# A fourth pair of token blocks takes the seven-product form in the first MLP

## The chip, the core and the metric

The kernel runs on one core of a Trainium2 chip. The metric is device time in microseconds, start to end of one execution, lower is better. A core has TensorE (PE in the profile, its weight loads are PEld), VectorE (DVE), ScalarE (ACT), GpSimd (POOL) and SyncE (SP, whose queue issues nearly all DMAs here), each with an instruction stream of its own that runs in order; streams wait for each other on semaphores.

## What is computed

Three stages on 6016 tokens of 256 channels, float32 throughout:

```python
qn = q / (norm(q, axis=tokens) + 1e-6); kn = k / (norm(k, axis=tokens) + 1e-6)
a  = softmax(kn.T @ qn / tau)              # 256 x 256
x  = v @ a                                 # attention
h  = maximum(x @ w_in, 0)                  # 256 -> 2048
x  = (h * h) @ w_out                       # first MLP, 2048 -> 256
xn = x / sqrt(mean(x * x) + 1e-6) * rms_g
out = (silu(xn @ w_gate) * (xn @ w_val)) @ w2   # second MLP, d_ff 1536
```

## The kernel before

Float32 products are made of three matmuls on high and low halves (high x high, high x low, low x high; `mm3`, L109 to L112). So every operand has to be split: ACT rounds to the high half, DVE subtracts to get the low half. Weights are also converted from their raw bits in several small steps (class `Call`: POOL and ACT in `a`, three DVE operations in `b0`, `b1`, `b2`, then `h` on ACT and `l` on DVE).

The attention matrix is folded into the first weight: M = a @ w_in, 256 x 2048, in halves m_h and m_l. `emit_m(fc)` makes M in eight parts of 256 columns, beside the first blocks. The first MLP is then relu(v @ M) squared, times w_out.

Tokens lie in 12 blocks: ten of 512 and two of 448. Two forms of the first MLP exist:

- **Ordinary blocks** (`mlp1`, L863). A block has 16 units, one for each 128 columns of M. In a unit PE makes `up(f)`: 6 matmuls into one of four banks; ACT takes relu (L870), a square (L874) and a rounded copy (L875), DVE subtracts for the low half (L882); where `act_heavy` is false the square is DVE's (L877) and ACT writes the rounded square at once (L878). Three units later PE makes `down(f)`, 6 matmuls into the block's sums. Blocks 0 and 1 are interleaved (32 units, numbered x), since the weights arrive meanwhile; later blocks follow one by one.
- **Pairs** (`mlp1_pair`, L1357). Two blocks together form the product with M from seven block products in place of eight (Strassen's scheme in Winograd's form). A pair has 8 groups; a group is 7 products of 3 matmuls and 24 matmuls of down. It needs sums of M's quarters (`comb_steps`, L1178) and seven operands made from the pair's v (`v_steps`, L1238).

`FIRST = NP - 3` (L56) puts blocks 0 to 5 into the ordinary form and pairs 3, 4 and 5 (blocks 6 to 11) into the other. The second MLP has the pair form for all six pairs.

All work beside PE's is placed by hand into units and groups. Lists by unit: `hooks` run ahead of the unit's relu, `beside` behind its subtraction. In blocks 2 to 4 (`CONV`) one conversion step (`conv_steps`) and at listed units one step of M's sums (`COMB`) stand beside each unit. `norm_steps(b)` (s0 to s6) is the RMS norm of a finished block, `pair_steps(p)` makes and stores the seven operands of the second MLP for a pair, `prep(b)` transposes and splits the next block's v. `third` (beside block 5) rounds the last of M's sums. In a pair, `aside()` runs after three of the products in each group: it takes one step from the list `side` (norms, `pair_steps`) and one from `tokens` (the next pair's `v_steps`); in the pair numbered FIRST a staged token step is held back where the side step just run was staged too (`staged` in `aside`).

`v_steps` has two forms. Pair FIRST + 1 goes through tiles vraw and vt. Later pairs are `wide`: their v is loaded (`load_v`, L465) at the end of the pair two before them into place p0 and the tile gv1, is worked on in gv1, and each operand goes through DRAM (v_dram). `fetch_v` brings an operand back: for a wide pair the first three into gv1, else into p6, vt and vraw; the other four into raw and dg.

Of the second MLP's gate and value weights a chunk (256 columns, seven operands) is 1.75 MB. Before, chunk 0 is converted in the blocks beside `CONV` and kept in gv0; chunk 1 (`STREAMED`) is converted beside the last pair (`last_chunk`), stored to DRAM and loaded into gv1 behind it.

Of the kernel before, what the change touches and what calls it, by code (L numbers as in the profile page):

```python
# [20 lines left out]
P = 128  # L21
NB = 512
# [6 lines left out]
def attn_moe_kernel(ctx: ExitStack, tc, q, k, v, tau, w_in, w_out, w_gate, w_val, w2, rms_g, out):  # L29
# [25 lines left out]
    NP = NBLK // 2  # L55
    FIRST = NP - 3  # L56

# [129 lines left out]
    NGV = F2 // W2  # L187
    HELD = 1
    EARLY = 1
# [6 lines left out]
    def gv_pool(i):  # L196
        return [(wp, "gv0"), (wp, "gv1"), (mp, "m_h"), (mp, "m_l"), (wp, "wo_h"), (wp, "wo_l")][i]

# [6 lines left out]
    class Pieces(Call):  # L205
# [5 lines left out]
        def direct(self):  # L211
            return self.i < HELD or self.i > STREAMED

# [77 lines left out]
    class Value(Pieces):  # L291
# [17 lines left out]
        def b2(self):  # L309
            super().b2()  # L310
            a2 = self.g.rearrange("p (k w) -> p k w", k=KC)
            s = self.raw.bitcast(F32).rearrange("p (c w) -> p c w", w=W2)
            self.pieces = [(a2[:, 1:], 2, 1), (s[:, :2], 3, 2), (s[:, 2:], 5, 2)]
            if self.i < STREAMED:
                for part in range(2):
                    self.sums(nc.gpsimd.tensor_tensor, part)
# [99 lines left out]

    gv_calls = [c for i in range(STREAMED) for c in chunk_calls(i)]
    w2_calls = [Rows2(rows2(w2, i), i) for i in range(EARLY)]
# [761 lines left out]
    def comb_steps():  # L1180
# [11 lines left out]
        def tt(o, a, b, op):  # L1192
            def f():
                if not comb:
                    tile3()
                x, y = (comb["t"][:, i] if isinstance(i, int) else m(*i) for i in (a, b))
                nc.vector.tensor_tensor(out=comb["t"][:, o], in0=x, in1=y, op=op)

            return f

        def hi(k, o):
            return lambda: nc.scalar.copy(out=comb["h"][:, k], in_=comb["t"][:, o])

        def lo(k, o):
            return lambda: nc.vector.tensor_tensor(
                out=comb["l"][:, k], in0=comb["t"][:, o], in1=f32(comb["h"])[:, k], op=ALU.subtract
            )
# [14 lines left out]
        ]  # L1222
        return steps, third

# [12 lines left out]
    def v_steps(p, into):  # L1237
# [7 lines left out]
        def loads(t):  # L1245
            def f():
                home = None
                if wide:
                    if t == 0:
                        x = wp.tile([P, NC7, NB], F32, tag="gv1", name="vx")  # L1250
                        st["raw"] = x[:, 5:]
                        st["x"] = {i: x[:, k, :n] for k, i in enumerate((0, 4, 2, 6, 3, 1, 5))}
                    home = (place(0, F32), st["raw"])[t]
                raw[t] = load_v(b + t, home)

            return f
# [90 lines left out]
    def fetch_v(p, i, ops):  # L1347

        n = blocks[2 * p][1]
        k = ORDER.index(i)  # L1350
        if k < 3 and p > FIRST + 1:
            if k == 0:
# [422 lines left out]
    ys = {b: parts[b][2] for b in (0, 1)}  # L1775
    n0, n1 = norm_steps(0, ys[0])
    for x, (b, f) in enumerate(order):
        up, down, _ = parts[b]
        beside = conv_steps(1) if x >= at0[NT] else ()
        unit(lambda: up(f), lambda down=down, f=f: down(f), 2 if x < 10 else 3, hooks.get(x, ()), late.get(x, ()), (), beside)  # L1780

    UNITS = 16
    CONV = range(2, 2 * FIRST - 1)

    cstep, third = comb_steps()
    SKIP = {2: (4, 10), 3: (4, 6, 9, 12), 4: (1, 5, 9, 11, 13)}
    COMB = {2: (2, 4, 6, 10, 14), 3: (0, 2, 12, 13, 14), 4: (2, 8, 9, 10, 11, 12)}


    ops1 = {}  # L1790
    spill = {}
    for b in range(2, 2 * FIRST):
        hooks, beside = spill, {}
        spill = {}

        if b == 2:
            hooks = merge({1: n0, 2: n1[:1], 3: n1[1:2], 4: n1[2:3]}, {6: n1[3:4], 7: n1[4:5], 8: n1[5:6], 9: n1[6:]})
            n0, n1 = norm_steps(1, ys[1])
            hooks = merge(hooks, {10: n0, 11: n1[:1], 12: n1[1:2], 13: n1[2:3]})
            spill = {0: n1[3:4], 1: n1[4:5], 2: n1[5:6], 3: n1[6:]}  # L1800
        else:
            n0, n1 = norm_steps(b - 1, ys[b - 1])
            if b == 2 * FIRST - 1:
                hooks = merge(hooks, *({u: [f]} for u, f in zip((8, 9, 10, 11, 13, 14, 15, 15), n0 + n1)))
            elif b % 2:
                hooks = merge(hooks, {13: n0, 14: n1[:1], 15: n1[1:2]})
                spill = {0: n1[2:3], 3: n1[3:4], 4: n1[4:5], 5: n1[5:6], 6: n1[6:]}
            else:
                hooks = merge(hooks, {7: n0, 8: n1[:1], 9: n1[1:2], 10: n1[2:3], 13: n1[3:4], 14: n1[4:5], 15: n1[5:]})
        if b > 2 and b % 2:  # L1810
            x = pair_steps(b // 2 - 1, staged("ys", "p0", "ys", "p1"))
            beside = merge(beside, at_steps(x, {3: 4, 2 * FIRST - 1: 0}.get(b, 1)))
        if b < 2 * FIRST - 1:
            x = prep(b + 1)
            hooks = merge(hooks, {0: [load(b + 1)]} if b > 2 else {})
            at = (8, 9, 12, 13) if b == 3 else (8, 9, 10, 11) if b % 2 else (3, 4, 8, 9)
            beside = merge(beside, {u: [f] for u, f in zip(at, x)})
        else:
            beside.setdefault(0, []).append(third)
            x = v_steps(FIRST, first_place(ops1))  # L1820
            for u in (0, 1, 3, 5, 6, 7, 8, 9, 10, 11, 11, 12, 13, 14, 15):
                beside.setdefault(u, []).append(x.pop(0))
        for u in range(UNITS):
            if b in CONV:
                if u not in SKIP.get(b, ()):
                    beside.setdefault(u, []).extend(conv_steps(1))
                if u in COMB.get(b, ()):
                    beside.setdefault(u, []).append(cstep.pop(0))
            beside.setdefault(u, []).append(lambda: None)
        up, down, ys[b] = mlp1(b, vts[b], (lambda f: f % 4 > 0) if b in CONV else (lambda f: f % 2 == 1))  # L1830
        run(up, down, NF1, 3, hooks, {}, beside)
        if b == CONV[-1]:
            left = [len(list(x)) for x in (conv, cstep)]
            assert left == [0, 0] and state["b"] == len(calls) == state["l"], left
# [65 lines left out]
    def last_homes():  # L1900
        halves = place(1, F32)
        last_chunk.update(
            chunk_steps(
                STREAMED,
                (
                    lambda: (as_raw(place(0, F32)), halves[:, 1]),
                    lambda: (as_raw(place(6, F32)), halves[:, 0]),
                ),
                None,
                lambda t=staged("p0", "vt"): t().rearrange("p a (c w) -> p a c w", w=W2),  # L1910
            )
        )
# [31 lines left out]
    side, tokens = [], []  # L1944
    drained.append(lambda: side.extend(n0 + n1 + pair_steps(FIRST - 1, first_stage)))
    first_stage = staged(*["ys", "p6", "ys"] * 4, "ys", "ys")
    for p in range(FIRST, NP):
# [9 lines left out]
        elif first:  # L1957
            tokens += v_steps(p + 1, through_dram(p + 1, stage))
            wide_steps = v_steps(p + 2, through_dram(p + 2, staged("p1", "p0")))
        else:  # L1960
            tokens += wide_steps

        def after_product(g, i):
            if g == NF1 // 2 - 1:
                if not last and i in ORDER[3:]:
                    fetch_v(p + 1, i, nxt)
                if last and i == 0:
                    fetch(0, 4, ops0, False)
                if p == FIRST and i == ORDER[-1]:
                    wide_steps.pop(0)()  # L1970
                    wide_steps.pop(0)()
                if p == NP - 2 and i == 0:
                    last_chunk["vload"]()

        def after_group(g):
# [4 lines left out]
            if not last and g == NF1 // 2 - 2:  # L1980
# [3 lines left out]
                if p == NP - 2:  # L1984
                    last_homes()
                    last_chunk["gload"]()
                    tokens.extend([bridge.a, bridge.b, None])
            if last:
                if g == NF1 // 2 - 3:
                    rows[f"{STREAMED + 1}gload"]()  # L1990
                if g == NF1 // 2 - 2:
# [52 lines left out]
    for i in range(STREAMED + 1, NGV):  # L2044
# [7 lines left out]

        if not early:
            add(f"{x}gload", (f"{j - 1}c", 0))
        add(f"{x}ga", (f"{x}gload", LAND), (f"{y}ve", 0), (f"{y}gl0", 0))
# [6 lines left out]
        for b, a, lag in (("b", "a", 2), ("c", "b", 1), ("h", "c", 2), ("l", "h", 1)):  # L2062
            add(f"{j}{b}", (f"{j}{a}", lag))
        if not early:
            add(f"{x}vload", (f"{y}vl2", 0))
        add(f"{x}va", (f"{x}vload", LAND), (f"{y}vl0", 0))
        for b, a, lag in (
# [3 lines left out]
            add(f"{x}{b}", (f"{x}{a}", lag), *([(f"{x}gc", 0)] if b == "vd" else [(f"{x}vl1", 0)] if b == "vl2" else []))  # L2071
    flow.at.update({f"{STREAMED + 1}gload": 0, f"{STREAMED + 1}vload": 0})
    side = []
# [10 lines left out]
    for x, (p, span) in enumerate(visits):  # L2084
# [7 lines left out]
        def after_group(f):  # L2092
            if x == 0:
                if f == 0:
                    load_w2(ROWS, 2)
                    rows[f"{STREAMED + 1}vload"]()
                if f == 1:
# [75 lines left out]
```

## Time and profile before

| | us |
|---|---|
| median of 3 executions | 1110.95 (1110.93 to 1111.2) |
| the profiled execution | 1110.91 |
| its span, first to last instruction | 1109.0 |
| PE busy | 1099.5 |
| DVE busy | 808.0 |
| ACT busy | 787.0 |

The profile shows one execution; times within it are counted from its first instruction. The busy time of PE counts the pipelined run of each matmul, so it says only that PE always has a matmul under way; how closely they follow each other is read from their starts.

### The profile page before, as it was taken

How to read it: one execution, taken by the hardware profiler on the slowest of the kernel's cores; microseconds unless marked ns; L12 is line 12 of the kernel's file. 1: busy time of each engine (PE TensorE's matmuls, PEld its weight loads, DVE VectorE, ACT ScalarE, POOL GpSimd, SP SyncE). 2: the span in 40 equal slices, each digit the busy share in tenths (PEclk: the TensorE clock that was granted, in tenths of full speed). 3: DMA queues.
4: the chain of work that ended last, by engine and by line, in shares of the span. 5: the costliest groups of instructions: out<-in, count | busy, mean ns of one | idle time of the engine just before them, and what ended most of it. 6: DMA issues, size and time to landing. Idle time of an engine off the chain costs nothing.

```text
span 1109.0 us, 14698 instructions
## 1 busy us (share of the span) xinstructions
PE 1099.5 (99%) x5148; PEld 928.0 (84%) x5148; DVE 808.0 (73%) x1266; ACT 787.0 (71%) x1430; POOL 39.1 (4%) x74
## 2 busy tenths in 40 slices
PE   9999999999999999999999999999999999999997
PEld 8978888888888888889988888888888888888996
DVE  7988768667777868979858888677556666565655
ACT  7888788787777778778777777676656555555554
POOL 2021101000000000000000000000000000000000
PEclk9999999999999999999999999999999999999999
DMA  9643210130411362461385656204323232404001
GB/s 346 214 114 96 87 47 20 48 105 1 135 56 58 143 219 50 152 253 39 129 325 226 226 197 220 72 9 169 133 73 133 77 133 54 149 21 122 20 20 33
DMA packets 113177, 130.98 MB, mean 118 GB/s; under 512 B 51664, under 2 KB 73168, under 8 KB 112976
## 3 DMA queue, kind: packets, MB, share of 16 engines
q1 hardware_dynamic: 110832, 129.20, 34.7%
q10 hardware_dynamic: 2272, 0.85, 0.3%
q8 instruction: 40, 0.66, 0.2%
q14 instruction: 33, 0.27, 0.1%
HBM read 87.43 MB, written 42.60 MB: 117 GB/s over the span
## 4 chain that ended last, share of the span: by engine, by line
PE 96%; DMA 2%; DVE 1%; SPq 1%; ACT 0%; issue 0%; DVEq 0%; ACTq 0%
PE mm L1548 30%; PE acc L111 13%; PE acc L110 13%; PE acc L112 13%; PE mm L1416 9%; PE mm L112 4%; PE mm L111 4%; PE mm L110 4%; PE mm L663 1%; PE acc L671 1%; PE acc L672 1%; PE acc L673 1%; PE mm L796 1%; DMA vr<-vd 1%; DMA qraw<-in_k_dram 0%; SPq L1163 0%
## 5 line engine op out<-in xcount | busy, mean ns | idle before, releaser
L1548 PE MATMUL mm<-p,gv 128*128 128x512 f32 (+1 forms) x1188 | 302.0, 387 | 0.0
L1548 PEld LDWEIGHTS mm<-p,gv 128*128 128x128 f32 x1188 | 222.0, 188 | 44.8 <-DVE hp L1628 1.0
L1653 DVE TENSOR_TENSOR sh<-hp,sh 128x512 fp32r<-128x512 f32 (+1 forms) x144 | 98.8, 686 | 111.8 <-ACT sh L1649 110.8
L1603 ACT COPY mm<-mm 128x512 f32<-128x512 f32 (+1 forms) x72 | 40.4, 562 | 159.7 <-PE mm L1548 154.9
L110 PE MATMUL acc<-sh,wo_h 128*128 128x512 f32 (+1 forms) x384 | 148.6, 387 | 0.0
L111 PE MATMUL acc<-sh,wo_h 128*128 128x512 f32 (+1 forms) x384 | 148.3, 386 | 0.1
L112 PE MATMUL acc<-sh,wo_l 128*128 128x512 f32 (+1 forms) x384 | 148.0, 385 | 0.0
L882 DVE TENSOR_TENSOR sh<-p,sh 128x512 fp32r<-128x512 f32 x96 | 67.1, 698 | 58.7 <-ACT sh L875 55.0
L110 PE MATMUL acc<-sh,w_h 128*128 128x512 f32 (+1 forms) x284 | 109.5, 385 | 0.0
L111 PE MATMUL acc<-sh,w_h 128*128 128x512 f32 (+1 forms) x284 | 109.5, 385 | 0.0
L112 PE MATMUL acc<-sh,w_l 128*128 128x512 f32 (+1 forms) x284 | 109.5, 385 | 0.0
L1649 ACT CAST sh<-hp 128x512 fp32r<-128x512 f32 (+1 forms) x144 | 89.0, 618 | 2.8 <-DVE hp L1637 1.9
L870 ACT ACTIVATE p<-mm 128x512 f32<-128x512 f32 x96 | 57.2, 596 | 41.7 <-PE mm L112 41.4
L111 PEld LDWEIGHTS acc<-sh,wo_h 128*128 128x128 f32 x384 | 72.1, 188 | 13.9 <-DVE sh L1406 0.7
L112 PEld LDWEIGHTS acc<-sh,wo_l 128*128 128x128 f32 x384 | 72.1, 188 | 13.6
L110 PEld LDWEIGHTS acc<-sh,wo_h 128*128 128x128 f32 x384 | 72.1, 188 | 13.3
L1548 PE MATMUL mm<-xs,gv 128*128 128x512 f32 (+1 forms) x324 | 82.6, 381 | 0.0
L1637 DVE TENSOR_TENSOR hp<-mm,sg 128x512 f32<-128x512 f32 (+1 forms) x72 | 48.8, 678 | 34.1 <-PE mm L1548 33.5
L1406 DVE TENSOR_TENSOR sh<-p,sh 128x512 fp32r<-128x512 f32 (+1 forms) x95 | 63.5, 668 | 13.7 <-ACT p L1401 5.5
L1548 PEld LDWEIGHTS mm<-xs,gv 128*128 128x128 f32 x324 | 60.8, 188 | 10.2
L1628 DVE TENSOR_TENSOR hp<-mm,pu 128x512 f32<-128x512 f32 (+1 forms) x72 | 48.9, 680 | 27.6 <-ACT pu L1627 27.5
L1397 ACT ACTIVATE sh<-p 128x512 fp32r<-128x512 f32 (+1 forms) x95 | 58.4, 615 | 9.3 <-DVE p L1466 7.3
(285 smaller groups left out, 2182.9 us busy)
## 6 DMA issues: line engine op xcount, KB each, us to landing
p<-xd SPq DMA_DIRECT2D x102, 256.0 KB, 4.6
xd<-xp SPq DMA_DIRECT2D x48, 256.0 KB, 2.2
xs<-xd SPq DMA_DIRECT2D x12, 512.0 KB, 5.8
xd<-p SPq DMA_DIRECT2D x22, 256.0 KB, 2.2
out_dram<-ot SPq DMA_DIRECT2D x40, 128.0 KB, 2.3
qraw<-in_q_dram SPq DMA_DIRECT2D x13, 384.0 KB, 7.1
qraw<-in_k_dram SPq DMA_DIRECT2D x13, 384.0 KB, 7.6
raw<-in_moe_w_out_dram SPq DMA_DIRECT2D x9, 512.0 KB, 3.5
```

Of the source, the lines that this page charges most:

```text
L110: nc.tensor.matmul(o, wh, xh, start=start, stop=False)
L111: nc.tensor.matmul(o, wh, xl, start=False, stop=False)
L112: nc.tensor.matmul(o, wl, xh, start=False, stop=stop)
L870: nc.scalar.activation(out=r, in_=o, func=AF.Relu)
L882: nc.vector.tensor_tensor(out=sl, in0=s, in1=f32(sh), op=ALU.subtract)
L1397: nc.scalar.activation(out=st["h"], in_=r, func=AF.Square)
L1406: nc.vector.tensor_tensor(out=st["l"], in0=q, in1=f32(st["h"]), op=ALU.subtract)
L1416: nc.tensor.matmul(bank, m_part(a, w, g), x, start=start and j == 0, stop=j == 2, skip_group_check=not start)
L1548: nc.tensor.matmul(bank, c[:, hl, a, fs], x, start=start and j == 0, stop=j == 2, skip_group_check=not start)
L1628: add(out=h22, in0=bh, in1=w, op=ALU.add)
L1649: nc.scalar.copy(out=parts[t][0], in_=x)
L1653: dve(out=pl, in0=x, in1=f32(ph), op=ALU.subtract)
```

## The change

FIRST becomes NP - 4: blocks 0 to 3 are ordinary, pairs 2 to 5 have the seven products. What stood beside blocks 2 to 5 has to go elsewhere:

- The sixteen steps of M's sums are split in halves of 512 columns (32 steps, `gs`). The first fourteen stand beside units x = 18 to 31 of blocks 0 and 1, the other eighteen beside block 2. All sixteen conversion steps are done by the end of block 2.
- Block 2 takes the norm of block 0 and three parts of four of block 1's; block 3 takes the rest of it, `pair_steps(0)` (through two staging tiles, `kept(2)`, in place of four), the beginning of block 2's norm, and pair 2's `v_steps`. The rest of block 2's norm (`kept_steps`) goes to the side list of pair 2.
- Pairs 4 and 5 are wide now; pair 4 has gv1 and pair 5 has gv0. So gv0 can't hold a chunk over the first MLP: chunk 1 is the one that is converted beside the blocks and goes through DRAM, into gv0 behind the last pair, and chunk 0 is converted beside the last pair, straight into gv1.
- Chunk 2's loads, which used vt and vraw (now operands of pair 5), move to the beginning of the second MLP.

```diff
-    FIRST = NP - 3
+    FIRST = NP - 4
...
-        return [(wp, "gv0"), (wp, "gv1"), (mp, "m_h"), (mp, "m_l"), (wp, "wo_h"), (wp, "wo_l")][i]
+        return [(wp, "gv1"), (wp, "gv0"), (mp, "m_h"), (mp, "m_l"), (wp, "wo_h"), (wp, "wo_l")][i]
...
-            return self.i < HELD or self.i > STREAMED
+            return self.i != STREAMED
...
-    gv_calls = [c for i in range(STREAMED) for c in chunk_calls(i)]
+    gv_calls = list(chunk_calls(STREAMED))
...
-            def f():
+            def f(gs):
                 if not comb:
                     tile3()
-                x, y = (comb["t"][:, i] if isinstance(i, int) else m(*i) for i in (a, b))
-                nc.vector.tensor_tensor(out=comb["t"][:, o], in0=x, in1=y, op=op)
+                x, y = (comb["t"][:, i, gs] if isinstance(i, int) else m(*i)[:, gs] for i in (a, b))
+                nc.vector.tensor_tensor(out=comb["t"][:, o, gs], in0=x, in1=y, op=op)
...
-        return steps, third
+        return [lambda f=f, gs=gs: f(gs) for gs in (slice(0, G // 2), slice(G // 2, G)) for f in steps], third
...
-                        x = wp.tile([P, NC7, NB], F32, tag="gv1", name="vx")
+                        x = wp.tile([P, NC7, NB], F32, tag=f"gv{(p - FIRST + 1) % 2}", name="vx")
...
-        if k < 3 and p > FIRST + 1:
+        if k < 3 and (p - FIRST) % 2 == 0:
...
+    cstep, third = comb_steps()
+    COMB0 = range(18, NU)
...
+        if x in COMB0:
+            beside = [*beside, cstep.pop(0)]
+            if x < at0[NT]:
+                beside.append(lambda: upto("h", state["b"]))
...
     for b in range(2, 2 * FIRST):
+        last = b == 2 * FIRST - 1
+        beside = {}
+        if not last:
+            n0, n1 = norm_steps(0, ys[0])
             hooks = merge({1: n0, 2: n1[:1], 3: n1[1:2], 4: n1[2:3]}, {6: n1[3:4], 7: n1[4:5], 8: n1[5:6], 9: n1[6:]})
             n0, n1 = norm_steps(1, ys[1])
             hooks = merge(hooks, {10: n0, 11: n1[:1], 12: n1[1:2], 13: n1[2:3]})
             spill = {0: n1[3:4], 1: n1[4:5], 2: n1[5:6], 3: n1[6:]}
+            beside = merge(beside, {u: [f] for u, f in zip((3, 4, 8, 9), prep(b + 1))})
+            for u in range(UNITS):
+                beside.setdefault(u, []).extend(conv_steps(1))
+                beside[u] += [cstep.pop(0) for _ in range(1 + (u in (5, 15)))]
         else:
...
+            n0, n1 = norm_steps(2, ys[2])
+            hooks = merge(spill, {13: n0, 14: n1[:1], 15: n1[1:2]})
+            kept_steps = n1[2:]
+            spill = {}
+            beside = merge(beside, at_steps(pair_steps(0, kept(2)), 4))
             beside.setdefault(0, []).append(third)
             x = v_steps(FIRST, first_place(ops1))
...
-        up, down, ys[b] = mlp1(b, vts[b], (lambda f: f % 4 > 0) if b in CONV else (lambda f: f % 2 == 1))
+        up, down, ys[b] = mlp1(b, vts[b], lambda f: f % 4 > 0)
...
-    drained.append(lambda: side.extend(n0 + n1 + pair_steps(FIRST - 1, first_stage)))
+    side.extend(kept_steps)
+    drained.append(lambda: (side.insert(0, n0[0]), side.extend(n1 + pair_steps(FIRST - 1, first_stage))))
...
+        if p + 2 < NP:
+            wide_steps = v_steps(p + 2, through_dram(p + 2, staged("p1", "p0")))
...
-                if p == FIRST and i == ORDER[-1]:
+                if p + 2 < NP and i == ORDER[-1]:
                     wide_steps.pop(0)()
                     wide_steps.pop(0)()
                 if p == NP - 2 and i == 0:
+                    last_homes()
+                    last_chunk["gload"]()
                     last_chunk["vload"]()
```

## Rows read from the trace of the kernel before

**Rows 1.** The page: span, busy time and share of PE, and the last chain.
```profile
span 1109.0 us, 14698 instructions
...
PE 1099.5 (99%) x5148; PEld 928.0 (84%) x5148; DVE 808.0 (73%) x1266; ACT 787.0 (71%) x1430; POOL 39.1 (4%) x74
...
PE 96%; DMA 2%; DVE 1%; SPq 1%; ACT 0%; issue 0%; DVEq 0%; ACTq 0%
```

**Rows 2.** Busy time by stretch: units x >= 18, blocks 2, 4, 5, pairs 3, 4.
```profile
core 0: us, PE busy (x) PEld busy (x) DVE busy (x) ACT busy (x) POOL busy (x), PEclk, DMA share, GB/s
112.37:153.37 41.00, 41.00 (x194) 34.41 (x192) 27.51 (x45) 31.36 (x54) 3.85 (x6) 1.00 0.27 77
153.37:197.14 43.77, 43.77 (x196) 36.27 (x195) 34.33 (x52) 37.23 (x65) 4.23 (x5) 1.00 0.09 25
...
240.90:284.92 44.02, 44.02 (x198) 36.49 (x197) 30.94 (x45) 31.80 (x55) 0.30 (x2) 1.00 0.00 1
284.92:328.68 43.76, 43.76 (x195) 36.27 (x194) 36.11 (x58) 34.70 (x61) 0.15 (x1) 1.00 0.38 121
328.68:410.63 81.95, 81.95 (x363) 67.65 (x362) 64.08 (x101) 62.09 (x112) 0.00 (x0) 1.00 0.33 118
410.63:492.92 82.29, 82.19 (x364) 67.68 (x363) 67.11 (x106) 63.43 (x114) 0.98 (x1) 1.00 0.44 151
```

**Rows 3.** Timeline of PE in block 4: start, duration; a norm's matmuls (L957) between.
```profile
249.97 0.39 PE L111 MATMUL mm<-p,m_h 128*128 128x512 f32 x1
250.20 0.39 PE L112 MATMUL mm<-p,m_l 128*128 128x512 f32 x1
250.42 0.29 PE L957 MATMUL mm<-ns,mean_w 128*128 128x16 f32 x2
250.56 0.48 PE L110 MATMUL acc<-sh,wo_h 128*128 128x512 f32 x1
250.88 0.40 PE L111 MATMUL acc<-sh,wo_h 128*128 128x512 f32 x1
```

**Rows 4.** Groups of DVE in block 2: count, busy us, mean ns, idle before.
```profile
L882 DVE TENSOR_TENSOR sh<-p,sh 128x512 fp32r<-128x512 f32 x16 | 11.4, 711 | 8.9 <-ACT sh L875 8.2
...
L1197 DVE TENSOR_TENSOR ct<-ct 128x1024 f32<-128x1024 f32 x1 | 1.8, 1757 | 0.0
...
L223 DVE TENSOR_TENSOR gv<-raw,gv 128x512 fp32r<-128x512 f32 x2 | 1.4, 684 | 0.0
...
L1197 DVE TENSOR_TENSOR ct<-m_h 128x1024 f32<-128x1024 f32 x1 | 1.2, 1218 | 0.0
```

**Rows 5.** The same of ACT in block 2.
```profile
L870 ACT ACTIVATE p<-mm 128x512 f32<-128x512 f32 x16 | 9.5, 596 | 4.8 <-PE mm L112 4.5
L874 ACT ACTIVATE p<-p 128x512 f32<-128x512 f32 x12 | 7.6, 633 | 0.4
L875 ACT CAST sh<-p 128x512 fp32r<-128x512 f32 x11 | 6.8, 622 | 0.4
...
L1202 ACT CAST ch<-ct 128x1024 fp32r<-128x1024 f32 x1 | 1.0, 1047 | 0.0
```

**Rows 6.** Timeline of DVE and weight loads at pair 4's second group; idle in brackets.
```profile
420.22 1.17 DVE L1267 STREAM_TRANSPOSE vx<-p 128x448 f32<-128x448 f32 x2 [1.57 <-DMA p<-in_v_dram]
...
421.31 0.65 DVE L1406 TENSOR_TENSOR sh<-p,sh 128x512 fp32r<-128x512 f32 x1
...
422.02 0.19 PEld L111 LDWEIGHTS acc<-sh,wo_h 128*128 128x128 f32 x1 [0.52 <-DVE sh L1406]
```

**Rows 7.** Timeline of SP's queue from pair 3 to pair 4.
```profile
402.65 2.23 SPq L1163 DMA_DIRECT2D p<-vd  x2
...
410.73 1.04 SPq L1365 DMA_DIRECT2D vd<-vd  x2
413.11 2.24 SPq L465 DMA_DIRECT2D p<-in_v_dram  x4
```

**Rows 8.** DMA issues: count, KB each, median us from issue to landing.
```profile
xd<-xp SPq DMA_DIRECT2D x48, 256.0 KB, 2.2
...
p<-in_v_dram SPq DMA_DIRECT2D x4, 112.0 KB, 5.5
```

More of the change, by code (lines that the diff above doesn't have):

```diff
@@ L187, in attn_moe_kernel @@
     NGV = F2 // W2
-    HELD = 1
     EARLY = 1
@@ L313, in b2 @@
             self.pieces = [(a2[:, 1:], 2, 1), (s[:, :2], 3, 2), (s[:, 2:], 5, 2)]
-            if self.i < STREAMED:
+            if self.i == STREAMED:
                 for part in range(2):
@@ L1192, in tt @@
         def tt(o, a, b, op):
-            def f():
+            def f(gs):
                 if not comb:
                     tile3()
-                x, y = (comb["t"][:, i] if isinstance(i, int) else m(*i) for i in (a, b))
-                nc.vector.tensor_tensor(out=comb["t"][:, o], in0=x, in1=y, op=op)
+                x, y = (comb["t"][:, i, gs] if isinstance(i, int) else m(*i)[:, gs] for i in (a, b))
+                nc.vector.tensor_tensor(out=comb["t"][:, o, gs], in0=x, in1=y, op=op)
             return f
         def hi(k, o):
-            return lambda: nc.scalar.copy(out=comb["h"][:, k], in_=comb["t"][:, o])
+            return lambda gs: nc.scalar.copy(out=comb["h"][:, k, gs], in_=comb["t"][:, o, gs])
         def lo(k, o):
-            return lambda: nc.vector.tensor_tensor(
-                out=comb["l"][:, k], in0=comb["t"][:, o], in1=f32(comb["h"])[:, k], op=ALU.subtract
+            return lambda gs: nc.vector.tensor_tensor(
+                out=comb["l"][:, k, gs], in0=comb["t"][:, o, gs], in1=f32(comb["h"])[:, k, gs], op=ALU.subtract
             )
@@ L1776, in attn_moe_kernel @@
     n0, n1 = norm_steps(0, ys[0])
+    cstep, third = comb_steps()
+    COMB0 = range(18, NU)
     for x, (b, f) in enumerate(order):
         up, down, _ = parts[b]
-        beside = conv_steps(1) if x >= at0[NT] else ()
+        beside = conv_steps(1) if x >= at0[NT] else []
+        if x in COMB0:
+            beside = [*beside, cstep.pop(0)]
+            if x < at0[NT]:
+                beside.append(lambda: upto("h", state["b"]))
         unit(lambda: up(f), lambda down=down, f=f: down(f), 2 if x < 10 else 3, hooks.get(x, ()), late.get(x, ()), (), beside)
     UNITS = 16
[L1783 to L1787, printed above, removed]
     ops1 = {}
@@ L1792, in attn_moe_kernel @@
     for b in range(2, 2 * FIRST):
-        hooks, beside = spill, {}
-        spill = {}
-        if b == 2:
+        last = b == 2 * FIRST - 1
+        beside = {}
+        if not last:
+            n0, n1 = norm_steps(0, ys[0])
             hooks = merge({1: n0, 2: n1[:1], 3: n1[1:2], 4: n1[2:3]}, {6: n1[3:4], 7: n1[4:5], 8: n1[5:6], 9: n1[6:]})
@@ L1800, in attn_moe_kernel @@
             spill = {0: n1[3:4], 1: n1[4:5], 2: n1[5:6], 3: n1[6:]}
-        else:
[L1802 to L1818, printed above, removed]
+            beside = merge(beside, {u: [f] for u, f in zip((3, 4, 8, 9), prep(b + 1))})
+            for u in range(UNITS):
+                beside.setdefault(u, []).extend(conv_steps(1))
+                beside[u] += [cstep.pop(0) for _ in range(1 + (u in (5, 15)))]
+        else:
+            n0, n1 = norm_steps(2, ys[2])
[3 more added lines that the diff above has]
+            beside = merge(beside, at_steps(pair_steps(0, kept(2)), 4))
             beside.setdefault(0, []).append(third)
@@ L1823, in attn_moe_kernel @@
         for u in range(UNITS):
[L1824 to L1828, printed above, removed]
             beside.setdefault(u, []).append(lambda: None)
-        up, down, ys[b] = mlp1(b, vts[b], (lambda f: f % 4 > 0) if b in CONV else (lambda f: f % 2 == 1))
+        up, down, ys[b] = mlp1(b, vts[b], lambda f: f % 4 > 0)
         run(up, down, NF1, 3, hooks, {}, beside)
-        if b == CONV[-1]:
+        if not last:
             left = [len(list(x)) for x in (conv, cstep)]
@@ L1900, in last_homes @@
     def last_homes():
-        halves = place(1, F32)
+        x = wp.tile([P, NC7, NB], F32, tag="gv0", name="cx")
         last_chunk.update(
[L1903 to L1911, printed above, removed]
+            chunk_steps(0, (lambda: (as_raw(x[:, 0:2]), x[:, 4]), lambda: (as_raw(x[:, 2:4]), x[:, 5])), None)
         )
@@ L1958, in attn_moe_kernel @@
             tokens += v_steps(p + 1, through_dram(p + 1, stage))
-            wide_steps = v_steps(p + 2, through_dram(p + 2, staged("p1", "p0")))
         else:
             tokens += wide_steps
+        if p + 2 < NP:
+            wide_steps = v_steps(p + 2, through_dram(p + 2, staged("p1", "p0")))
         def after_product(g, i):
@@ L1984, in after_group @@
                 if p == NP - 2:
-                    last_homes()
-                    last_chunk["gload"]()
                     tokens.extend([bridge.a, bridge.b, None])
             if last:
-                if g == NF1 // 2 - 3:
-                    rows[f"{STREAMED + 1}gload"]()
                 if g == NF1 // 2 - 2:
@@ L2051, in add @@
             flow.add(name, rows[name], *after)
-        if not early:
-            add(f"{x}gload", (f"{j - 1}c", 0))
+        add(f"{x}gload", *([] if early else [(f"{j - 1}c", 0)]))
         add(f"{x}ga", (f"{x}gload", LAND), (f"{y}ve", 0), (f"{y}gl0", 0))
@@ L2063, in attn_moe_kernel @@
             add(f"{j}{b}", (f"{j}{a}", lag))
-        if not early:
-            add(f"{x}vload", (f"{y}vl2", 0))
+        add(f"{x}vload", (f"{y}vl2", 0))
         add(f"{x}va", (f"{x}vload", LAND), (f"{y}vl0", 0))
@@ L2071, in attn_moe_kernel @@
             add(f"{x}{b}", (f"{x}{a}", lag), *([(f"{x}gc", 0)] if b == "vd" else [(f"{x}vl1", 0)] if b == "vl2" else []))
-    flow.at.update({f"{STREAMED + 1}gload": 0, f"{STREAMED + 1}vload": 0})
     side = []
@@ L2095, in after_group @@
                     load_w2(ROWS, 2)
-                    rows[f"{STREAMED + 1}vload"]()
                 if f == 1:
```

## Prediction

> **What bounds the kernel now.** I read the page first. PE is busy for 1099.5 of a span of 1109.0 us and carries 96% of the chain that ended last [rows 1]; DVE and ACT have a quarter of the span idle. So the time is PE's instruction count times its pace, plus what PE waits. The pace is read from starts: two 512-column matmuls follow each other at 249.97 and 250.20, and the next instruction at 250.42, so 0.227 us each (0.39 is the pipelined duration, not the pace) [rows 3]. What PE waits is read stage by stage: an ordinary block has 16 units of 12 matmuls, 192 x 0.227 = 43.58 us, and blocks 2 and 5 take 43.77 and 43.76 [rows 2], which leaves 0.18 to 0.19; a pair has 8 groups of 45, 360 x 0.227 = 81.72 us, and pairs 3 and 4 take 81.95 and 82.29, which leaves 0.2 and 0.6. PE's clock is granted in full (1.00) in all of these rows, the upper of its two levels, 2.4 GHz. So PE streams nearly without gaps in both forms, and a matmul that goes is worth its 0.227 us, as long as DVE and ACT keep up with what is now put beside fewer blocks.
>
> **The change part by part.**
>
> *Fewer matmuls.* Blocks 4 and 5 now make 360 matmuls where two ordinary blocks make 384: 24 x 0.227 = 5.45 us less, all on the path. Downs, M, the last pair and the second MLP keep their counts.
>
> *One norm less on PE.* A norm's two small matmuls take 250.42 to 250.56, and the next matmul takes 0.32 instead of 0.227: 0.14 + 0.09 = 0.23 us [rows 3]. Six norms of blocks and three of pairs become four and four: 0.23 us less. Together 5.68 us. The stage rows agree: blocks 4 and 5 together take 87.78, pair 4, with its own gap, 82.29 [rows 2], 5.5 less.
>
> The Trainium skill (TensorE: Matmul & The Clock Gate, Back-to-back issue gap) gives a sustained spacing of about 131 ns for 512 columns. By it the 24 matmuls would be worth 3.1 us instead of 5.45. The trace disagrees: 0.227 us in a stretch without gaps [rows 3], so the sum goes by the trace.
>
> *Work beside units x = 18 to 31.* Of the 32 half steps of M's sums the first fourteen come here: eleven on DVE, three on ACT. A full step of 1024 columns takes 1.22 us, an operation of 512 columns 0.68 [rows 4], so a half step is taken as 0.68 on DVE; on ACT, by the 512-column copy, 0.62 [rows 5]. DVE is busy 27.51 of 41.00 us there [rows 2]; 11 x 0.68 = 7.5 makes 35.0. It fits. At its fullest, x = 24 and 25 where conversion, v's steps and a part of M meet, I count DVE some 1.5 us behind, and an M part is used two units after it is made. Cost nothing.
>
> *Work beside block 2.* The conversion steps and both norms are about those that stand there now. Five full steps of the sums go (three of them and the low half at 1.2, one at 1.76 that ran beside POOL's sums: 5.4 us of DVE, one copy of 1.05 on ACT) and eighteen half steps come, fifteen on DVE (10.2 us) and three on ACT (1.9). DVE: 34.33 - 5.4 + 10.2 = 39.1 of 43.77 us; ACT: 37.23 - 1.05 + 1.9 = 38.1 [rows 2, 4, 5]. That is 89% and 87%: it fits as a whole, and what counts is the worst run of units. That is units 3 and 4: two transposes, the norm's add, transpose and reduction, three DVE operations of a conversion, two half steps, a square and both subtractions, 9.5 us in two units of 2.72, so DVE is about 4 us behind. What covers it: down(f) comes six half units (8.2 us) behind the end of up(f), and the chain relu, square, copy, subtraction takes 0.60 + 0.63 + 0.62 + 0.71 = 2.6, some 2.8 with its gaps [rows 4, 5]. So 5.3 us can be lost before PE notices, and DVE, which waits 8.2 us for ACT in this block [rows 4], starts a unit with part of its backlog free. I take 0; the bounds are 0 and 2.5 us.
>
> *Work beside block 3.* It takes over block 5's tokens and third, with pair_steps(0), less of a norm, and the square on ACT in three units of four. ACT by count: relu 16 x 0.60, squares and copies 12 x 1.25 + 4 x 0.63, fourteen roundings at 0.62, third 1.05, norms 2.7, in all 39.5 of 43.8 us; DVE less than block 5's 36.11 [rows 2, 5], as four squares leave it. A new wait: with two staging tiles a rounding on ACT waits until the tile's last store has landed, 2.2 us after its issue [rows 8]. A low half is formed a unit ahead, some 4.9 us after that unit's start, so it lands at 4.9 + 2.2 - 2.7 = 4.4 us into the next unit; ACT reaches the rounding at about 3.5. It may wait 1 us, and relu, square and copy of the next unit queue behind it; the 5.3 us cover that. Nothing; bounds 0 and 1 us.
>
> *Pair 2* is pair 3 of before with five more side steps (about 3 us of DVE in 82). Nothing by itself.
>
> *A second wide pair.* This is what costs. Where pair 4 begins, its next wide operands' v is queued on SP behind the fetches: issued at 413.11 [rows 7], landing 5.5 us later [rows 8]; the DVE transposes wait 1.57 us for it, the subtraction behind them comes late, and PE's weight load waits 0.52 us (0.37 lost) at 422.02 [rows 6]. After the change this happens twice. In pair 4, for pair 5, as now: no difference. In pair 3, for pair 4, it is new, with 512 tokens: 128 KB a load for 112, and two transposes of 0.70 for 0.58. So the 0.37 is there once more, plus 0.24 of transposes, plus a few tenths for the later landing: 0.9 us. Bounds 0 (the loads land before the transposes' turn) and 2.5 (the wait of 1.57 plus 0.9).
>
> The Trainium skill (DMA: Bandwidth & Descriptors, HWDGE ordering) says that one issuing queue has one ring on each DMA engine, consumed in ring order. By that rule the v loads come behind all fourteen fetches whatever their size, and the stall is there again. The landing of 5.5 us against 2.2 for a store elsewhere [rows 8] agrees.
>
> *Chunks 0 and 1* change places. The conversion is the same; four stores go from the last pair to block 2, where the DMA engines are 9% busy [rows 2]. Chunk 2's loads come later, and are due only many groups later. Nothing, 0.3 either way.
>
> Sum: -5.45 - 0.23 + 0.9 = -4.8 us on the profiled execution's 1110.91, which is 0.04 from the median: 1106.1.
>
> **The rivals.**
>
> *The boundary from pair 2 to pair 3 stalls.* Pair 2's side list has 21 steps for 16, and where a staged side step runs a staged token step is held back, so the last two of pair 3's v steps slip toward the eighth group. Their store lands late, the fetch of that operand waits for it on SP, and the v loads behind it. For it: SP's queue is full there from 402.65 on [rows 7]. Against it: the other fetches go ahead meanwhile, and the data move in the same total time. Price: a slip of one third of a group (3.4 us) at most, 1.5 to 3.4 us: 1107.6 to 1109.5.
>
> *DVE becomes the bound (slower).* If DVE keeps its idle time ahead of the subtractions (8.9 us in block 2, 8.2 of it for ACT [rows 4]) though it has 39.1 us of work, block 2 needs 48 us, and units 18 to 31 with 35.0 and waits of the same size per unit 42.8 for 41.0. That is 4.2 + 1.8 = 6.0; ACT, held by the two tiles of squares that DVE frees late, adds as much as its own idle in block 2 (43.77 - 37.23 = 6.5). Together 12.5; less the 5.3 of cover, 7.2 us are lost in block 2. Time: 1106.1 + 7.2 = 1113.3. It decides from a backlog of 5.3 us on. Against it: a wait for ACT is idle time of an engine that is ahead, and shrinks when it is behind.
>
> *The pace of the page.* If a matmul less were worth only 131 ns, 3.1 in place of 5.45: 1108.5. That the change does not do what it says can only take this form, since the count of matmuls is fixed.
>
> **How the numbers follow.** Forecast 1106.1 with its bounds (stalls 0 to 2.5 in place of 0.9): chance 0.78. Boundary: 0.14. DVE: 0.06. Pace: 0.02. The forecast alone runs from 1105.2 (no new stall) to 1107.8; taking in most of the boundary, and 0.3 below for the chunks, 1104.9 to 1109.3. A difference under 0.2%, 2.2 us, can't be told from none here, so faster means under 1108.7: all of the forecast, the pace, and five of the boundary's fourteen hundredths: 0.85. Same 0.09, slower 0.06.
>
> **What would show it.** Right: 24 fewer 512-column matmuls; PE starts 0.227 us apart; blocks 2 and 3 at 43.8 us each; pairs 2, 3, 4 at 82 to 83; a PE wait for L1406 near the second group of pair 3, larger than the one of now. Wrong: gaps of PE behind L882 in block 2 (DVE or ACT bound), PE waiting on a fetched operand in the first group of pair 3 (boundary), or a second MLP that is longer than now.

## The result, and the profile after

| | before | after |
|---|---|---|
| median, us | 1110.94 | 1116.63 (1115.77 to 1117.2, four runs) |
| profiled execution: span | 1109.0 | 1115.0 |
| PE instructions | 5148 | 5122 |

The ratio is 1.0051, 95% interval 1.0033 to 1.0068: slower by half a per cent, where 1106.1 had been forecast. The page of the changed kernel answers to [rows 1]:

```profile
span 1115.0 us, 14668 instructions
...
PE 1097.9 (98%) x5122; PEld 923.7 (83%) x5122; DVE 828.1 (74%) x1305; ACT 787.8 (71%) x1441; POOL 57.8 (5%) x72
```

The 24 matmuls and the norm's two are gone (5148 - 5122 = 26). Where the time went is seen in the busy time by stretch: units x >= 18, blocks 2 and 3, then pairs 2, 3 and 4, the same columns as in [rows 2]:

```profile
112.37:153.37 41.00, 41.00 (x194) 34.40 (x193) 32.83 (x54) 32.61 (x58) 3.72 (x6) 1.00 0.27 78
153.37:197.14 43.77, 43.77 (x196) 36.26 (x195) 40.05 (x64) 37.63 (x67) 4.54 (x5) 1.00 0.20 67
197.14:241.21 44.07, 44.07 (x197) 36.49 (x196) 33.27 (x53) 37.15 (x65) 0.15 (x1) 1.00 0.33 108
241.21:334.54 93.33, 86.15 (x365) 68.43 (x364) 67.48 (x108) 61.78 (x113) 0.15 (x1) 0.98 0.29 105
334.54:417.28 82.74, 82.26 (x364) 67.66 (x362) 67.48 (x104) 63.25 (x113) 0.00 (x0) 1.00 0.43 150
417.28:499.17 81.89, 81.89 (x363) 67.74 (x362) 67.33 (x105) 63.31 (x114) 0.66 (x1) 1.00 0.43 147
```

The first three stretches begin 0.3 us before the units and blocks they are named for (the marks are those of [rows 2]); blocks 2 and 3 take 43.8 each, as they did. Pair 2 takes 93.33 us, 11.4 more than the first pair of before (81.95 [rows 2]); pairs 3 and 4 take 82.74 and 81.89. Without these 11.4 us the span would be 5.4 shorter than before; with them it is 6.0 longer.

Which engine starts it is read from the groups of ACT within pair 2: the roundings of `pair_steps(1)` (L1099) and of pair 3's `v_steps` (L1279), with count, busy time, mean and the idle time before them:

```profile
L1099 ACT CAST xp<-xst 128x512 fp32r<-128x512 f32 x5 | 3.1, 621 | 11.0 <-DMA xd<-xp 7.3 <-DVE p L1110 1.9 <-DVE sh L1405 1.8
L1279 ACT CAST xp<-p 128x512 fp32r<-128x512 f32 x3 | 1.8, 604 | 0.0
L1279 ACT CAST xp<-vt 128x512 fp32r<-128x512 f32 x2 | 1.2, 613 | 3.4 <-DVE p L1402 3.4
```

ACT stands idle ahead of these for 14.4 us. Beside pair 3 of before the same roundings waited 0.3 us in all:

```profile
L1100 ACT CAST xp<-xst 128x512 fp32r<-128x512 f32 x4 | 2.4, 610 | 0.3 <-DMA vd<-xp 0.3
L1280 ACT CAST xp<-p 128x512 fp32r<-128x512 f32 x4 | 2.4, 608 | 0.0
```

They wait for the tile into which they round. The timeline shows one such wait as it begins and ends, and then the whole chain to PE at the pair's end (start, duration; idle before in brackets):

```profile
301.49 0.68 DVE L1110 TENSOR_TENSOR xp<-xst,xp 128x512 fp32r<-128x512 f32 x1
302.20 0.32 SPq L1111 DMA_DIRECT2D xd<-xp  x1
304.24 0.62 ACT L1099 CAST xp<-xst 128x512 fp32r<-128x512 f32 x1 [3.65 <-DMA xd<-xp]
...
317.40 0.62 ACT L1099 CAST xp<-xst 128x512 fp32r<-128x512 f32 x1 [3.66 <-DMA xd<-xp]
318.60 0.49 PE L110 MATMUL acc<-sh,wo_h 128*128 128x512 f32 x1 [1.13 <-ACT sh L1396]
319.85 0.50 PE L111 MATMUL acc<-sh,wo_h 128*128 128x512 f32 x1 [0.75 <-DVE sh L1405]
322.08 0.32 SPq L1111 DMA_DIRECT2D xd<-xp  x1
324.14 0.62 ACT L1279 CAST xp<-vt 128x512 fp32r<-128x512 f32 x1 [3.41 <-DVE p L1402]
325.30 0.50 PE L1415 MATMUL mm<-vx,ch 128*128 128x512 f32 x1 [3.34 <-ACT mm L1441]
```

DVE forms a low half at 301.49, SP issues its store at 302.20, the rounding starts when the store has landed, 2.0 us later. ACT runs in order, so the relus, squares and bank copies behind the rounding wait as well, and then PE. (The last wait is put down to DVE L1402, which had ended at 323.3; the store issued at 322.08 needs the 2 us.)

Why a tile is short: the two lists share three staging tiles, two of ys and p6. Pair 3's operand 6 is rounded into one of the ys tiles at 285.25. Its low half and store come 37 us later:

```profile
285.25 0.61 ACT L1279 CAST xp<-p 128x512 fp32r<-128x512 f32 x1
...
321.98 0.68 DVE L1287 TENSOR_TENSOR xp<-p,xp 128x512 fp32r<-128x512 f32 x1
322.69 0.32 SPq L1342 DMA_DIRECT2D vd<-xp  x1
```

In `v_steps` that low half shares a step with the rounding of operand 5 (`seq(lo(6), hi(5))`), which makes it a staged step, and in pair FIRST a staged token is held back wherever a staged side step has just run. Five side steps more put the first step of `pair_steps` just between the rounding of operand 6 and its low half. From there on seven roundings share one ys tile and p6.

### The profile page after: what moved, and what is told of

Its sections match the earlier page's. It is cut to its first block, busy times and chain, and to the rows that moved or that the text cites. A ratio compares the mean times of both kernels' runs of the same rounds, so it can differ in the third digit from the quotient of the medians.

```text
span 1115.0 us, 14668 instructions
## 1 busy us (share of the span) xinstructions
PE 1097.9 (98%) x5122; PEld 923.7 (83%) x5122; DVE 828.1 (74%) x1305; ACT 787.8 (71%) x1441; POOL 57.8 (5%) x72
## 4 chain that ended last, share of the span: by engine, by line
PE 69%; DMA 1%; DVE 0%; SPq 0%; issue 0%; ACT 0%; DVEq 0%
PE mm L1547 30%; PE mm L1415 10%; PE acc L111 10%; PE acc L112 10%; PE acc L110 10%; DMA p<-in_v_dram 1%; PE acc L1679 0%; SPq L464 0%; SPq L1364 0%; SPq L1162 0%; DVE sh L1405 0%; DVE vx L1266 0%; DVE xp L1110 0%; DVE ot L1693 0%; DVE hp L1636 0%
## 5 line engine op out<-in xcount | busy, mean ns | idle before, releaser
L1405 DVE TENSOR_TENSOR sh<-p,sh 128x512 fp32r<-128x512 f32 (+1 forms) x127 | 85.8, 676 | 28.0 <-ACT p L1400 12.5
L1396 ACT ACTIVATE sh<-p 128x512 fp32r<-128x512 f32 (+1 forms) x127 | 78.6, 619 | 11.5 <-DVE p L1465 8.4
L1402 DVE TENSOR_TENSOR p<-p 128x512 f32<-128x512 f32 (+1 forms) x79 | 53.3, 674 | 32.7 <-ACT p L1457 32.6
L881 DVE TENSOR_TENSOR sh<-p,sh 128x512 fp32r<-128x512 f32 x64 | 45.2, 706 | 27.5 <-ACT sh L874 25.3
```

The costliest lines, as they stand in the source:

```text
L1396: nc.scalar.activation(out=st["h"], in_=r, func=AF.Square)
L1402: nc.vector.tensor_tensor(out=q, in0=r, in1=r, op=ALU.mult)
L1405: nc.vector.tensor_tensor(out=st["l"], in0=q, in1=f32(st["h"]), op=ALU.subtract)
```

## Experiments

The theory after the result: **the held tile**. The rival: **the place**, that the side steps simply come too late, into the groups where SP fetches the next pair's operands; and for one run **the load**, that what was moved into blocks 2 and 3 does it. Four runs tell them apart.

**x1: free the low half alone.**

```diff
-            seq(lo(2), hi(6)), seq(lo(6), hi(5)), lo(5),
+            seq(lo(2), hi(6)),
+            *([seq(lo(6), hi(5))] if p == FIRST else [lo(6), hi(5)]), lo(5),
```

> The changed kernel, with one step of pair 3's v steps cut in two: the low half of operand 6 and its store no longer share a step with the rounding of operand 5, so they aren't held back behind the staged side steps. Theory (held tile): that low half holds one of the three staging tiles from 288 to 323 us, pair_steps(1) has two tiles left, and ACT waits for a store to land four times; with the tile free pair 2 takes about 82.3 us instead of 93.3 and the kernel 1106.0 to 1107.0. Rival (place): the side steps simply come too late, in the last groups, where they meet the fetches; they stay where they are here, so 1113 or more.

Measured: 1107.49 (ratio to the kernel before 0.997, interval 0.9961 to 0.998). Pair 2 takes 82.97 us, and its roundings wait 0.3:

```profile
240.77:323.74 82.97, 82.61 (x365) 67.77 (x364) 67.39 (x108) 62.46 (x113) 0.15 (x1) 1.00 0.31 110
```
```profile
L1099 ACT CAST xp<-xst 128x512 fp32r<-128x512 f32 x5 | 3.1, 620 | 0.3 <-DMA vd<-xp 0.3
```

The order of the side steps is untouched, so the place is not the cause. (The list of v steps is one longer, which matters at the next boundary.) The time is 0.5 above what the theory allowed; what is left lies at that boundary, below.

**x4: leave the order, give the side list its own tiles.**

```diff
-    drained.append(lambda: (side.insert(0, n0[0]), side.extend(n1 + pair_steps(FIRST - 1, first_stage))))
+    drained.append(lambda: (side.insert(0, n0[0]), side.extend(n1 + pair_steps(FIRST - 1, side_stage))))
...
+    def side_stage():
+        if not thirds:
+            x = wp.tile([P, NC7, NB], F32R, tag="gv0", name="sx")
+            thirds.extend(cycle([x[:, 2 * i : 2 * i + 2] for i in range(3)]) for _ in range(1))
+        return next(thirds[0])
```

> The changed kernel, where pair_steps(1) takes its staging tiles from gv0, which is free in pairs 2 and 3, and the v steps keep theirs; all steps stay where they are and the low half is still held. Theory (held tile): no rounding waits for a store, pair 2 takes 82 to 82.5 us, 1105.8 to 1106.8. Rival (place): 1113 or more.

Measured: 1107.91 (ratio 0.9973, 0.9962 to 0.9983). The low half is still held, yet the seven roundings wait for nothing:

```profile
L1099 ACT CAST sx<-xst 128x512 fp32r<-128x512 f32 x7 | 4.3, 614 | 0.0
```

So the tile is the cause, from the other side. The time is 1.1 us above the expected range; pair 2 takes 82.97 us here too, above the 82 to 82.5 expected, and the rest lies in pair 3:

```profile
323.32:408.17 84.85, 82.69 (x363) 67.52 (x362) 67.47 (x104) 63.28 (x113) 0.00 (x0) 1.00 0.44 156
```

**x3: only the slip, in the kernel before.**

```diff
-    drained.append(lambda: side.extend(n0 + n1 + pair_steps(FIRST - 1, first_stage)))
+    drained.append(lambda: side.extend(n0 + n1 + [None] * 3 + pair_steps(FIRST - 1, first_stage)))
```

> The kernel before, with three empty places in pair 3's side list ahead of pair_steps(2): nothing is added or left out, those eight steps only come three places later, as in the changed kernel. Theory (held tile): the rule now holds the same low half, so pair 3 loses what pair 2 lost, 8 to 11 us: 1119 to 1122. Rival (load): the loss comes from what was moved into blocks 2 and 3 and the norm steps left over from them; nothing of that is here, so 1111 to 1112.

Measured: 1122.04, 10.9 us above the kernel before (ratio 1.0105, 1.009 to 1.012). Three empty places reproduce the loss with nothing added, so the load is not needed for it. Pair 3 takes 90.7 us (the stretch below begins 0.2 us before it), 8.8 more than before, and pair 4 another 1.4 more; ACT's waits are those of the changed kernel:

```profile
329.40:420.34 90.94, 85.54 (x364) 68.26 (x363) 64.28 (x102) 61.66 (x112) 0.00 (x0) 0.98 0.28 101
```
```profile
L1100 ACT CAST xp<-xst 128x512 fp32r<-128x512 f32 x5 | 3.1, 620 | 10.9 <-DMA xd<-xp 5.5 <-issue 3.6 <-DVE sh L1406 1.8
L1280 ACT CAST xp<-vt 128x512 fp32r<-128x512 f32 x2 | 1.2, 610 | 3.4 <-DMA xd<-xp 3.4
```

Here the wait of 3.4 us ahead of the last rounding is put down to the store, which supports the attribution above.

**x2: no hold-back rule.**

```diff
-                        if p == FIRST and staged and getattr(q[0], "staged", False):
-                            break
```

> The changed kernel without the rule that holds a staged token step back behind a staged side step. Theory (held tile): no low half is held, the three tiles go round, 1106.0 to 1107.5 (two roundings in one aside may cost a few tenths). Rival (place): the side steps are where they were, 1113 or more. Rival (density): the rule was needed, since two roundings at once keep ACT from PE's banks; then pair 2 loses 3 us or more elsewhere, 1109 or more.

Measured: 1105.64 (ratio 0.9955, 0.994 to 0.997). That is 0.4 below the expected range, and both rivals fail: neither the place nor two roundings at once cost what they were said to. The side list's roundings in pair 2 still wait 1.8 us for stores, and PE loses 0.4 us in the pair's sixth group. The pairs 2, 3 and 4:

```profile
240.84:324.34 83.50, 83.17 (x365) 67.53 (x364) 67.29 (x108) 62.07 (x113) 0.15 (x1) 1.00 0.34 124
324.34:406.29 81.95, 81.95 (x363) 67.76 (x362) 67.58 (x104) 63.17 (x113) 0.00 (x0) 1.00 0.41 145
406.29:488.18 81.89, 81.89 (x363) 67.76 (x362) 67.44 (x105) 63.42 (x114) 0.66 (x1) 1.00 0.42 146
```

What x1 and x4 lose against it lies in pair 3. In x1 it takes 85.5 us, in x4 84.9 (81.95 in x2):

```profile
323.74:409.26 85.52, 82.76 (x363) 67.51 (x362) 67.38 (x104) 63.29 (x113) 0.00 (x0) 1.00 0.44 153
```

The timeline of x1 where pair 3 begins, DVE's transposes of the next wide pair's v and the PE wait behind them, and SP's queue ahead of it:

```profile
336.40 1.31 DVE L1266 STREAM_TRANSPOSE vx<-p 128x512 f32<-128x512 f32 x2 [4.50 <-DMA p<-in_v_dram]
338.33 0.50 PE L111 MATMUL acc<-sh,wo_h 128*128 128x512 f32 x1 [2.21 <-DVE sh L1406]
```
```profile
319.07 0.43 SPq L1343 DMA_DIRECT2D vd<-xp  x1
319.61 7.45 SPq L1162 DMA_DIRECT2D vr<-vd  x6
327.10 0.91 SPq L1365 DMA_DIRECT2D vd<-vd  x2
328.05 2.37 SPq L464 DMA_DIRECT2D p<-in_v_dram  x4
```

The last v step has slipped into the last group and its store goes out between the fetches (319.07). It lands 7.1 us later; SP waits 2.9 us for that before it can issue the last fetches, so that the six behind it take SP 7.45 us, and v is issued at 328.05, 4.3 us after the pair's start; DVE waits 4.50 us for it and PE 2.2. In x2 the stores are out in time, the six fetches take SP 4.20 us, v is issued 0.1 us after the pair's start, and PE loses nothing:

```profile
319.13 4.20 SPq L1162 DMA_DIRECT2D vr<-vd  x6
323.37 0.91 SPq L1364 DMA_DIRECT2D vd<-vd  x2
324.47 2.79 SPq L464 DMA_DIRECT2D p<-in_v_dram  x4
```

That is the boundary rival of the prediction. In the profiled executions pair 3 takes 3.6 us (x1) and 2.9 us (x4) more than in x2; by the medians the whole kernels take 1.9 and 2.3 us more.

**x5: the same edit in the kernel before**, as a control for x2.

> The kernel before without the hold-back rule: the control for the same edit in the changed kernel. If the rule protects the kernel before, it gets slower here; if the rule only delays the last store of pair 4's operands, the fetches and the wide load behind it land earlier and pair 4's gap of 0.37 us goes, with two to four tenths lost where two roundings meet: 1110.5 to 1111.3. Either way the seventh-product pair by itself is then this time less that of the changed kernel without the rule (1105.64): 5.0 to 5.7 us by the sum of the prediction without its stall (5.45 + 0.23).

Measured: 1118.11 (ratio 1.0062, 1.0045 to 1.0079): 6.7 us slower than the kernel before run beside it (1111.37), far above the range that I had given. What I had named first, without a price, is what came: the rule does protect the kernel before. There `pair_steps` begins while three roundings of the v steps are still to come, and without the rule both lists draw on the three tiles at every `aside`. The group of v steps that waited 0.0 us beside pair 3 of before now waits 3.7 for landings, and with the other roundings of both lists it is 9.4 us:

```profile
L1280 ACT CAST xp<-p 128x512 fp32r<-128x512 f32 x4 | 2.5, 613 | 3.7 <-DMA xd<-xp 2.2 <-DMA vd<-xp 1.4
```

The other half of the expectation came as well: the gap of 0.37 us in pair 4 is gone (81.89 us). In the changed kernel only one rounding of the v steps is left when `pair_steps` begins, so the rule has little to protect, and holds a tile instead. This run is no base for the gain of the fourth pair, which it had been meant for.

**x6: both edits, no rule and tiles of gv0.**

> The changed kernel without the hold-back rule and with gv0's staging tiles for pair_steps(1): no rounding of pair 2 has to wait for a landing from either list. Against the rule's removal alone (1105.64) the 0.43 us that pair 2 still lost in its sixth group should go: 1105.1 to 1105.5. If that gap is two roundings in a row on ACT and no wait for a tile, it stays: 1105.6.

Measured: 1105.07 (ratio 0.9945, 0.993 to 0.9959), just below the expected range, and the fastest of all. The loss in pair 2's sixth group is gone, so it was a wait for a tile. Pairs 2, 3 and 4 take 82.96, 81.92 and 81.90 us:

```profile
240.41:323.37 82.96, 82.62 (x366) 67.77 (x364) 67.39 (x108) 62.16 (x113) 0.15 (x1) 1.00 0.34 124
323.37:405.29 81.92, 81.92 (x363) 67.74 (x362) 67.61 (x104) 63.18 (x113) 0.00 (x0) 1.00 0.41 146
405.29:487.19 81.90, 81.90 (x364) 67.74 (x362) 67.30 (x106) 63.32 (x114) 0.66 (x1) 1.00 0.43 146
```

The change itself does what it says: 5.9 us less than the kernel before's 1110.94 (6.3 less than its median beside this run). Not all of that is the change. From block 2 to the end of pair 4 this execution takes 334.3 us (152.87 to 487.19) and the kernel before 339.6 (153.37 to 492.92 [rows 2]), 5.2 less; another 0.5 lies ahead of unit 18, where executions differ as much (block 0's first matmul comes at 58.0 to 58.8 us in the changed kernel and its variants, whose edits all take effect later). The sum says 5.7 for the matmuls and the norm, and 0.4 for the wait where pair 4 began [rows 6], which is gone; against that, pair 2 is still 1.0 us longer than pair 3 of before. It has one norm more (0.23 us; the sum counts norms over all stages), and about 0.6 us goes in its fifth group, where PE waits for a low half. The changed kernel has the same gap, and so have x1, x2 and x4:

```profile
284.13 0.50 PE L111 MATMUL acc<-sh,wo_h 128*128 128x512 f32 x1 [0.35 <-DVE sh L1405]
```

DVE's steps of the second norm stand just ahead of it. That they are the reason was not tested.

**x7: how much block 2 can bear.** On x2, one more operation of DVE in each unit of block 2.

```diff
+    def extra():
+        if not spare0:
+            spare0.append(wp.tile([P, NC7, NB], F32, tag="gv0", name="xx"))
+        i = f32(m_h)[:, 0, :NB]
+        nc.vector.tensor_tensor(out=spare0[0][:, 0], in0=i, in1=i, op=ALU.add)
...
+                beside[u].append(extra)
```

> The changed kernel without the hold-back rule, with one more addition of 512 columns on DVE in each of block 2's 16 units (into gv0, read by nobody): about 9.8 us more of DVE work in a block of 43.8 us, to find how much block 2 can bear. Cover theory: DVE then has 48 to 49 us of work, ends the block some 5 us behind, its waits for ACT vanish, and PE loses 0 to 1.5 us: 1105.6 to 1107.2. Rival (DVE keeps its waits for ACT): PE loses 5 us or more: over 1110.6.

Measured: 1108.09, 2.45 us above x2 (2.2 when each is read against the kernel before run beside it, 1111.37 and 1111.13), between the two. Block 2 takes 46.04 us (43.77 in x2) with DVE busy for 45.10, and the idle time ahead of the low halves is 0.7 us for fifteen of them, where it was 3.4 in x2 and 8.9 in the kernel before [rows 4]:

```profile
152.89:198.93 46.04, 45.46 (x195) 35.79 (x194) 45.10 (x73) 36.74 (x66) 4.53 (x5) 1.00 0.19 63
```
```profile
L881 DVE TENSOR_TENSOR sh<-p,sh 128x512 fp32r<-128x512 f32 x15 | 10.8, 719 | 0.7
```

So DVE's waits go when it is behind, as the cover says, but not without loss: DVE was busy for 98% of the block, and the block went at its pace. Thirteen of the sixteen additions, 10.0 us, ran within the block; the other three ran behind it, and block 3 took no longer for them (43.78 us).

## Why the prediction was wrong

**The step that failed** is "Pair 2 is pair 3 of before with five more side steps (about 3 us of DVE in 82). Nothing by itself." The pair costs 11.4 us more in the changed kernel. With the tile free (x1, x4, x6) 1.0 is left, so 10.4 are the held tile's, with what it did to PE's clock. And the 1.0 is not nothing either: 0.6 of it is the gap in the fifth group. I counted the work of the five steps and not what their places do to the steps behind them. All that was needed stood in the code: three tiles for two lists, a rounding that takes a tile until its low half has been stored, and a rule that may hold the step with that low half. I had weighed exactly this wait for block 3, where two tiles stand in for four, and had the landing time for it (2.2 us [rows 8]); I did not put the same question to pair 2.

**The boundary rival** had the slip right ("the last two of pair 3's v steps slip toward the eighth group") and what it does to SP's queue; x1 and x4 show it at 2.9 to 3.6 us in the profiled executions and at 1.9 to 2.3 by the medians, about its price of 1.5 to 3.4. It looked only at the fetches, not at what a held step keeps occupied.

**Fewer matmuls, one norm less**: right. 26 PE instructions less, PE at 0.227 us, 5.2 us less in the stages of x6 that the change touches, with pair 2's 0.6 against it. The upper end of the forecast was added up as 1107.8; 1105.2 and 2.5 make 1107.7. The spacing of 131 ns in the Trainium skill (TensorE: Matmul & The Clock Gate, Back-to-back issue gap) is contradicted once more: by it the 24 matmuls, the norm and the wait of pair 4 would make an estimated 3.7 us (3.1 + 0.23 + 0.37), and 5.2 were gained in spite of the 0.6.

**Units 18 to 31, block 2, block 3**: right, without a gap of PE. In the stretches shown above DVE in units 18 to 31 was put at 35.0 us and is 32.83; in block 2 at 39.1 and is 40.05; ACT in block 2 at 38.1 and is 37.63; ACT in block 3 at 39.5 and is 37.15. The slower rival there did not come: DVE's idle time ahead of the low halves shrank from 8.9 [rows 4] to 3.4 us:

```profile
L881 DVE TENSOR_TENSOR sh<-p,sh 128x512 fp32r<-128x512 f32 x16 | 11.8, 737 | 3.4 <-ACT sh L874 2.6
```

x7 adds how far this cover reaches: 10 us more of DVE in block 2 cost 2.2 to 2.45.

**The second wide pair**: in the changed kernel the wait for the load is there in pair 3, as forecast, and 0.8 us in size for 0.9; in pair 4 it is gone. In x2 and x6 it is in neither, and in x5 pair 4 loses it too. So it was never a price of wide pairs: it hangs on how early the last v store leaves. That 0.8 came near 0.9 is luck.

**Chunks 0 and 1**: nothing to be seen, as taken.

None of my cases had the slower time by its true cause; the chance of 0.06 for slower stood on DVE in block 2.

## What to carry to other kernels

When steps move in a hand-made order, follow what each one keeps occupied (a staging tile, a bank) from its first half to its last, not only its time; a rule that holds back one half of such a pair is safe only in the order for which it was made. On an engine that runs in order, a rounding that waits 3.6 us for a tile stops all that the bottleneck is fed by, though the engine is idle a quarter of the time. A tile that is free anyway (gv0 here) ends the waits for a tile, but not a late store: by itself it left the kernel at 1107.91 (x4), without the rule at 1105.07 (x6), and the rule's removal alone at 1105.64 (x2).

## What the runs showed of the hardware

After the long waits PE did not only lose the waits. The changed kernel from 315 us on, with the columns of [rows 2] (PE's busy time second, its granted clock third from the end):

```profile
315.00:320.00 5.00, 3.11 (x13) 2.03 (x13) 1.22 (x3) 2.57 (x5) 0.00 (x0) 1.00 0.27 105
320.00:325.00 5.00, 1.95 (x8) 1.27 (x8) 2.89 (x5) 1.59 (x4) 0.00 (x0) 1.00 0.44 156
325.00:327.50 2.50, 2.20 (x7) 1.78 (x8) 1.29 (x2) 1.88 (x4) 0.00 (x0) 0.75 0.67 215
327.50:330.00 2.50, 2.50 (x8) 1.92 (x8) 0.62 (x1) 1.22 (x2) 0.00 (x0) 0.57 0.68 205
```

PE was busy 5.1 of 10 us up to 325; then the granted clock fell to 0.75 and 0.57 on average, near the lower of its two levels, 1.2 GHz, while PE worked without a gap. The starts show it:

```profile
326.38 0.63 PE L111 MATMUL acc<-sh,wo_h 128*128 128x512 f32 x1
326.81 0.63 PE L112 MATMUL acc<-sh,wo_l 128*128 128x512 f32 x1
327.23 0.63 PE L1415 MATMUL mm<-vr,m_h 128*128 128x512 f32 x1
```

They are 0.43 us apart instead of 0.227. Seven starts follow at that distance, and one at 0.37; together they make 1.55 of the 11.4 us. In x1 a single wait of 2.2 us had no such sequel: the mean clock of its pair 3 is 1.00.
